# Linear attention and a squared-ReLU MLP on one core: padded v tails, paired tail divisions, fewer last stores, a second matmul by halves, a new order

## Chip, cores and metric

The kernel runs on one core of one Trainium2 chip. The metric is the device time of one execution in microseconds (us). The engines are TensorE (PE, with its weight loads shown as PEld), VectorE (DVE), ScalarE (ACT), GpSimd (POOL) and SyncE (SP). SP, ACT and POOL also issue DMAs.

## What is computed

```python
def _attn_ref(q, k, v):                  # 8 batches, 8 heads, 576 positions, 64 columns
    theta = np.pi / 2.0 * np.arange(S) / S
    cos_w, sin_w = np.cos(theta), np.sin(theta)
    phi = lambda x: concat([max(x, 0) * cos_w, max(x, 0) * sin_w], axis=-1)
    q_p, k_p = phi(q), phi(k)
    kv = np.einsum('bhsf,bhsd->bhfd', k_p, v)
    z = np.sum(k_p, axis=2)
    num = np.einsum('bhsf,bhfd->bhsd', q_p, kv)
    den = np.einsum('bhsf,bhf->bhs', q_p, z)[..., None] + 1e-06
    return num / den

def _moe_ref(x, w_in, w_out):            # 4608 tokens, 512 -> 2048 -> 512
    r = np.maximum(x @ w_in, 0.0)
    return (r * r) @ w_out
```

The attention's result, with the heads side by side, is the input x of the MLP. Inputs and output are float32; the matmuls run on bfloat16.

## The kernel before

**Tiling.** The 576 positions of a batch are 512 main ones (four tiles of 128, j = 0 to 3) and a tail of 64. The main positions of a batch go through the MLP as two token blocks of 256. The eight tails, 512 tokens, are gathered and go through the MLP as a ninth batch, number 8 in the names. In a tail tile heads 0 to 3 lie in partitions 0 to 63 and heads 4 to 7 in partitions 64 to 127.

**Stages of a batch.** Loads of q, k and v (`ldq`, `ldk`, `ldv`, and `ldqt`, `ldkt` for tails); features (`cos`, `sin`, with `.t` for the tail) into `fe` and `fet`; v cast to bfloat16 beside a column of ones (`vs`, into `vext` and, for the tail, `vextt`), so that one matmul gives kv and z; the sums (`kv`, into `kz` in PSUM, then copied to `kvz`); the transposed features of q (`qTd` by a DMA transpose, or `qT` and `qTc` by PE and a copy for batches 0 and 1) into `qpT` and `qpTt`; the numerators (`num`) and the division (`div`: add epsilon, reciprocal, multiply) into `xp` and `xpt`; and the transpose of x (`xTd` or `xT`, `xTc`) into `xT` and, for the tails, `xTt`.

**The MLP.** The first matmul is `H` (plain: batches 0 and 1 and half of batch 2) or `G` (a seven-product scheme after Strassen and Winograd, with sums `xs` of x blocks and `w1s` of weights). Its results are clipped (`...r`) and squared (`...q`) into `gT`. The second matmul is `Y0` (plain, batch 0) or `Yb` (seven products `P1` to `P7`, sums `S1` to `S4`, copies `seed`, `u2`, `s5`, results `c11` to `c22`, stores `st`).

**The order.** All of this is recorded first as named operations with the buffers that they use. Then the table `ORDER` (lines 23 to 116) is walked: it says in which order they are written out, and a star puts an operation on ACT instead of DVE. Each engine, and each DMA queue, runs its own instructions in that order. Buffers come from small pools (`pool(...)`): an operation that needs a new buffer is held until the last user of the old one is done. A pool of one, such as `pool("qpTt", 1, 1024)`, `pool("fet", 1, 2048)` and `pool("xpt", 1, 512)`, ties one batch to the one before it. SP's queue carries nearly all loads from batch 3 on, all DMA transposes and the stores; half of the very last stores are on ACT's.

**Lines that the change touches.** `mm_kv` (the tail is a matmul of 64 rows for each head: `fet[b][p0:p1, ...]` by `vxt[p0:p1, ...]`), `mm_num` (the tail's result fills 64 partitions for each half of the heads, in one PSUM bank), `div`, `spread_v` (v's casts), `x_dma`, `plan_q`, `plan_first2` (`Y0`: sixteen contraction blocks, each with four token tiles of 128), `store` and `plan_pair` with `apart=True` (the last `Y8`: 16 stores of 64 KB, in groups of two token tiles, two halves of heads, two column halves and two row blocks). All matmuls go through the helper `mm`, so they all carry its line, L459, and are told apart by their tiles.

Of the kernel before, what the change touches and what calls it, by code (L numbers as in the profile page):

```python
# [23 lines left out]
qT0.2 xT0.k2 xT0.k3 xTc0.k3* H0.0.00.0 xTc0.k2* qT0.3 qTc0.3* qTc0.2 num0.2 H0.0.00.1 H0.0.00.2  # L24
div0.2 H0.1.00.0 H0.1.00.1 H0.1.00.2 num0.3 div0.3 xT0.2 H0.0.00r* H0.3.00.0 H0.2.00.0 xT0.3
xTc0.3 xTc0.2* H0.0.01.0 H0.0.01r* H0.3.10.0 H0.3.10r H0.2.10.0 f0.t1* H0.0.10.0 H0.0.10r*
ldv2.0 H0.2.01.0 H0.2.01r* f0.t0 qT0.4 H0.2.00r* H0.1.00r H0.1.10.0 H0.1.10r* H0.1.10q H0.1.01.0
H0.0.11.0 H0.1.11.0 H0.1.01r* H0.1.00q qTc0.4* num0.4 H0.2.10r* H0.0.11r H0.3.00r* H0.2.11.0
H0.3.00q* H0.2.11r H0.3.01.0 H0.3.11.0 H0.3.01r* H0.1.11r H0.1.01q* Y0.0 sin1.t* div0.4 xT0.4
Y0.1 Y0.2 Y0.3 cos1.t* xTc0.4 H0.3.11r* qT1.4 qTc1.4* cos1.0 sin1.0* sin1.2 cos1.2* H0.3.10q  # L30
Y0.4 Y0.5 Y0.6 cos1.1 vs1.1* sin1.1 qT1.0 qTc1.0* cos1.3 Y0.7 vs1.0 sin1.3 qT1.3 qTc1.3* vs1.2
kv1 qT1.1 qTc1.1* qT1.2 H0.1.11q Y0.8 ldv2.2 w1s1 H0.3.11q* ldk2 ldq2 w1s2 ldkt2.0 ldkt2.1 kvz1
num1.1 ldkt3.0 div1.1 w2t1 qTc1.2* ldqt3.1 Y0.9 Y0.10 ldqt2.0 xT1.1 num1.2 Y0.11 div1.2 ldqt2.1
H0.3.01q* Y0.12 xTc1.1* w2t2 num1.0 div1.0 xT1.2 xTc1.2* vs2.2* ldkt3.1 Y0.13 Y0.14 num1.3
div1.3 vs2.0* xT1.0 xTc1.0* ldv3.2 Y0.15 H1.3.00.0 Y0.c11 Y0.c10* H1.3.00r* Y0.c00* ldv2.1
# [6 lines left out]
H1.2.11r* H1.3.11q Y1.S1 H1.3.01.0 Y1.P1 H1.3.01r* H1.3.01q* num2.0 div2.0 xTd2.0 Y1.S2 Y1.seed
Y1.P2 Y1.c11* num1.4 div1.4 Y0.st1 cos3.0 Y1.P6 sin3.1 Y1.S3 cos3.1* qTd2.2 sin3.0* qTd3.0
sin3.3 cos3.3* cos3.2* sin3.2 qTd3.1 vs3.1* Y1.P5 Y1.s5 xs2.1 Y1.S4 H2.1.10.0 H2.1.10r* sin3.t
ldk4 ldv4.0 ldkt4.0 H2.0.00.0 H2.0.01.0 H2.0.00r* H2.0.01r* xs2.2 G2.2.P1 H2.1.00.0 H2.1.00r*
H2.1.00q* cos3.t H2.0.11.0 ldq4 w1s4 Y1.u2* H2.0.11r xs2.4 kv3 G2.2.seed kvz3* vs4.2* ldv5.2
ldqt4.1 H2.1.11.0 xs2.3 w2t4 G2.2.P2 G2.2.c11r* num3.0 div3.0 H2.1.01.0 H2.1.01r* H2.1.01q
H2.1.11r* H2.1.11q* H2.0.10.0 H2.0.10r* ldkt4.1 num3.1 xT1.4 Y1.P7 H2.1.10q* div3.1 w1s3 xTd3.0
num3.2 div3.2 Y1.P3 vs4.0* G2.2.P5 G2.2.s5* num3.3 ldqt4.0 Y1.c22 Y1.c12 xTc1.4 G2.2.P6 G2.2.u2*
div3.3 G2.3.P1 G2.2.P3 G2.2.c12r G2.3.seed ldv4.1 G2.2.P7 sin4.0* num2.4 G2.3.P6 G2.3.u2* sin4.3  # L50
G2.3.P2 G2.3.c11r* G2.3.P5 G2.3.s5* xTd3.1 Y1.P4 qTd3.2 cos4.0 cos4.1 sin4.1 qTd4.0 G2.3.P7
G2.3.c11q G2.3.P3 Y1.st0 sin4.2* cos4.3* cos4.2* Y2.P1 G2.2.c22r G2.2.P4 cos4.t* G2.3.c22r
G2.3.P4 div2.4 Y1.c21* vs4.1 G2.3.c21r* qTd4.1 G3.0.P1 sin4.t kv4 G3.0.seed G2.2.c21r* kvz4*
ldv5.0 xs3.1 xs3.2 Y2.seed G3.0.P5 G2.3.c12r G2.3.c12q G3.0.P2 G3.0.c11r* xs3.4 ldq5 G2.3.c21q
G3.0.P6 G3.0.u2 xs3.3 G3.1.P1 G3.1.seed num4.0 div4.0 ldqt5.0 Y2.P2 G2.3.c22q* Y2.S1 G3.0.P7
G3.0.s5* G3.0.c22r G3.1.P2 G3.1.c11r* G3.1.P6 G3.0.P3 ldk5 Y2.S2 G3.1.u2* num4.2 div4.2 G3.0.P4
G3.1.P7 G3.1.P5 G3.0.c21r* Y2.S3 G3.0.c12r xTd2.2 G3.2.P1 Y2.P6 ldkt5.0 G3.1.c11q* num4.1
Y2.c11* div4.1 Y2.S4 ldkt5.1 Y2.P5 Y1.st1 vs5.0* G3.1.s5* G3.1.P3 G3.1.c12r num4.3 G3.1.c22r
ldqt7.0 div4.3 xTd4.0 Y2.u2* G3.2.P5 G3.2.s5* Y2.P7 G3.2.seed ldv5.1 G3.1.P4 Y2.s5* cos5.0*
G3.2.P6 sin5.3* G3.2.P2 G3.2.c11r* sin5.1 G3.1.c21r num3.4 G3.3.P1 cos5.1 cos5.2 Y2.P3 G3.3.seed  # L60
G3.3.P2 G3.3.P6 G3.2.u2* ldqt5.1 sin5.2 G3.2.P7 cos5.3 G3.1.c21q* Y2.c12 G3.3.u2* G3.3.c11r*
xTd4.1 G3.3.P5 Y2.c22 Y2.P4 G3.1.c22q* G3.3.s5* G3.1.c12q* sin5.0 qTd4.2 G3.2.c22r G3.2.P4
div3.4 G3.3.c11q qTd5.1 qTd5.0 vs5.1 ldv6.0 G3.3.P7 G3.3.c22r G3.2.P3 G3.2.c12r G3.3.P3
G3.3.c12r Y2.c21* G3.2.c21r* G4.0.P1 G4.0.seed G3.3.P4 Y3.P1 xs4.1 xs4.2 G4.0.P6 xs4.4
G3.3.c21r* G3.3.c21q* cos5.t* sin5.t G4.0.u2* G4.0.P5 G4.0.s5* vs5.2 G4.1.P1 xs4.3 G4.1.seed
G3.3.c12q G3.3.c22q kv5 Y3.S1 kvz5* ldkt7.1 G4.0.P3 G4.0.c12r G4.0.P2 G4.0.c11r* ldq6 num5.0
div5.0 G4.1.P6 G4.1.u2* G4.0.P7 G4.0.c22r G4.1.P5 Y3.seed G4.1.P7 vs6.0* Y3.S2 Y2.st1 G4.1.P2
num5.2 ldqt6.0 div5.2 ldk6 Y3.P2 G4.1.s5* G4.1.c22r ldkt6.1 G4.1.P3 num5.3 div5.3 Y3.c11* Y3.P6
G4.1.c11r* Y3.u2* cos6.2* G4.2.P1 G4.1.c11q* Y3.S4 G4.0.P4 G4.0.c21r Y3.P5 Y2.st0 ldkt6.0 Y3.S3
num5.1 div5.1 ldv6.1 G4.1.P4 G4.1.c21r* Y3.s5* G4.1.c12r G4.2.P5 xTd3.2 Y3.P7 G4.2.seed G4.2.s5  # L70
cos6.1* num4.4 G4.2.P3 xTd5.1 G4.1.c21q* G4.3.P1 G4.2.P2 G4.2.c11r* G4.2.P6 G4.1.c22q Y3.c22
Y3.P4 div4.4 G4.2.u2* G4.2.P7 G4.3.seed G4.3.P6 ldqt6.1 sin6.1 Y3.c21* G4.3.u2* cos6.0 sin6.2*
G4.1.c12q ldv6.2 G4.3.P5 sin6.3 qTd5.2 G4.3.P2 sin6.0 G4.3.P7 ldqt7.1 Y3.P3 cos6.3 vs6.2 G4.3.s5
xTd5.0 qTd6.0 G4.3.c11r* sin6.t G4.3.P3 vs6.1* cos6.t* qTd6.1 G4.2.c22r G4.2.P4 G4.3.c11q*
G4.3.c22r G4.2.c12r Y3.c12 G4.3.P4 G5.0.P1 G4.2.c21r* G5.0.seed kv6 xs5.1 Y3.st0 G4.3.c21r
G4.3.c21q* G5.0.P5 xs5.2 G5.0.P6 ldv7.0 G5.0.P2 kvz6* G5.0.s5* G4.3.c22q G5.0.c11r* G4.3.c12r
Y4.P1 Y4.seed num6.0 G5.0.u2 Y3.st1 G5.1.P1 G5.0.P3 Y4.P2 G4.3.c12q Y4.S1 Y4.S2 div6.0 G5.1.seed
G5.1.P2 G5.1.c11r* xTd4.2 vs7.0* G5.1.P6 G5.1.u2* xs5.3 num6.1 G5.0.P7 Y4.P6 Y4.S4 G5.1.c11q*
G5.1.P7 div6.1 Y4.S3 num6.2 xs5.4 ldk7 div6.2 ldq7 Y4.c11* G5.1.P5 G5.1.s5* Y4.u2* Y4.P5 Y4.s5*
# [203 lines left out]
def kernel(  # L283
# [812 lines left out]
    def plan_pair(b, apart=False):  # L1096
# [117 lines left out]
        for t in range(2):  # L1214
            plan_store(b, key, ys[1], 1, [e22], t, 1)
# [312 lines left out]
```

## Time and profile before

| | |
|---|---|
| median of 3 runs | 275.24 us (274.66 to 276.22) |
| the profiled execution | 275.57 us |
| its span, first to last instruction | 273.0 us |
| granted TensorE clock | 0.998 |
| PE busy | 265.0 us, 97% |
| DVE busy | 227.2 us, 83% |
| ACT busy | 186.9 us, 68% |
| last dense matmul starts in the group at | 267.16 us |
| DMA moved | 53.00 MB, mean 194 GB/s |

All times below count from the start of the span. PE's matmuls overlap in the pipeline: what a group costs is read from its start to the start of the next. "Idle before" stands in brackets with the instruction that ended it. A group's name is its output tile, an arrow, and its inputs: `kz<-vextt,fet` is the tail part of kv, `num<-kvz,qpTt` a tail numerator.

### The profile page before, as it was taken

The page shows a single profiled execution, that of the slowest core. Times are in us where ns is not written, and L with a number is a line of the kernel's source. Part 1 is how long each engine was busy: PE and PEld are TensorE (multiplying, and loading weights), DVE is VectorE, ACT ScalarE, POOL GpSimd, SP SyncE. Part 2 cuts the span into 40 slices and gives each one's busy share as a digit, 9 for nine tenths or more (in the row PEclk, how much of TensorE's full clock was granted, in tenths as well). Part 3 has the DMA queues.
Part 4 walks back from the last instruction along what each step waited for, and adds up shares of the span by engine and source line. Part 5 has one row for each costly group of instructions (what it writes and reads, how often), then busy time and mean ns, then how long its engine had stood idle before and what let it go on. Part 6 is the DMA issues. An engine that isn't in the chain of part 4 may idle for free.

```text
span 273.0 us, 6796 instructions
## 1 busy us (share of the span) xinstructions
PE 265.0 (97%) x2788; PEld 225.0 (82%) x2792; DVE 227.2 (83%) x412; ACT 186.9 (68%) x287; POOL 29.1 (11%) x47
## 2 busy tenths in 40 slices
PE   8999999999999989999999999999999999999992
PEld 3578756798899878989888998889988888888882
DVE  2773598897999989999999998998979979788931
ACT  5673888788699878699668866997249355747510
POOL 8934437100000000000000000000000000000000
PEclk9999999999999999999999999999999999999999
DMA  7999999999999999999993999573150010100125
GB/s 223 311 206 271 317 284 319 297 248 346 197 274 326 184 254 262 345 227 259 366 204 88 271 323 246 145 208 46 41 192 4 10 77 3 79 0 2 74 70 166
DMA packets 79198, 53.00 MB, mean 194 GB/s; under 512 B 52256, under 2 KB 74784, under 8 KB 79168
## 3 DMA queue, kind: packets, MB, share of 16 engines
q1 hardware_dynamic: 71488, 38.28, 55.3%
q0 software_dynamic: 7040, 13.76, 19.0%
q10 hardware_dynamic: 640, 0.52, 0.7%
q8 instruction: 22, 0.36, 0.6%
q14 instruction: 8, 0.07, 0.1%
HBM read 36.70 MB, written 9.44 MB: 169 GB/s over the span
## 4 chain that ended last, share of the span: by engine, by line
PE 91%; ACT 2%; DMA 2%; POOL 2%; issue 1%; DVE 0%; POOLq 0%; ACTq 0%
PE ya L459 19%; PE yb L459 15%; PE hps L459 13%; PE hb L459 12%; PE hc L459 8%; PE ha L459 8%; PE yh L459 5%; PE num L459 4%; PE kz L459 3%; DMA v<-in_v_dram 2%; PE yc L459 1%; PE tq L609 1%; ACT fe L446 1%; PE tx L614 1%; PE wm L459 1%
## 5 line engine op out<-in xcount | busy, mean ns | idle before, releaser
L459 PEld LDWEIGHTS <-w1sb 128*128 128x128 bf16 x736 | 70.6, 98 | 8.7 <-DMA w1sb<-in_moe_w_in_dram 0.2
L459 PEld LDWEIGHTS <-gs 128*128 128x128 bf16 x512 | 49.7, 98 | 5.7
L459 PEld LDWEIGHTS <-gT 128*128 128x128 bf16 x448 | 43.3, 98 | 10.3 <-issue 0.5
L440 ACT ACTIVATE gT<-gT 128x1024 bf16<-128x1024 bf16 x39 | 41.1, 1058 | 3.0 <-DVE gT L453 2.7
L459 PE MATMUL hps<-xT,w1sb 128*128 128x256 bf16 x320 | 37.6, 273 | 0.0
L459 PEld LDWEIGHTS <-w1s 128*128 128x128 bf16 x312 | 29.7, 98 | 4.2 <-issue 0.6
L448 DVE TENSOR_SCALAR fe<-kq,cols 128x1024 bf16<-128x1024 f32 (+1 forms) x43 | 28.8, 712 | 4.1 <-DMA kq<-in_k_dram 4.1
L459 PE MATMUL ya<-w2sb,gT 128*128 128x256 bf16 x256 | 30.7, 273 | 0.4 <-ACT yb L430 0.4
L459 PE MATMUL hb<-xs,w1sb 128*128 128x256 bf16 x208 | 30.1, 272 | 0.0
L446 ACT ACTIVATE fe<-kq,cols 128x1024 bf16<-128x1024 f32 (+1 forms) x29 | 28.7, 1032 | 2.0 <-DMA kq<-in_k_dram 2.0
L459 PE MATMUL ha<-xT,w1sb 128*128 128x256 bf16 x176 | 25.8, 273 | 0.0
L442 DVE TENSOR_TENSOR gT<-gT 128x1024 bf16<-128x1024 bf16 x33 | 22.1, 686 | 2.8 <-ACT gT L434 2.6
L591 DVE TENSOR_TENSOR xp<-num,den 128x512 bf16<-128x512 f32 (+1 forms) x33 | 22.2, 675 | 1.1
L453 DVE CUSTOM_DVE_ANT_0 gT<-hb,s 128x512 bf16<-128x512 f32 x26 | 17.6, 687 | 5.3 <-PE hb L459 5.0
L434 ACT ACTIVATE gT<-hps 128x512 bf16<-128x512 f32 x30 | 17.0, 597 | 6.7 <-PE hps L459 6.6
L434 ACT ACTIVATE gT<-ha 128x512 bf16<-128x512 f32 x23 | 13.8, 601 | 9.9 <-PE ha L459 9.9
L456 DVE TENSOR_TENSOR gs<-gT 128x2048 bf16<-128x2048 bf16 x16 | 19.5, 1220 | 0.7 <-ACT gT L440 0.2
L453 DVE CUSTOM_DVE_ANT_0 gT<-hc,u 128x512 bf16<-128x512 f32 x26 | 17.5, 684 | 1.1 <-PE hc L459 0.7
L430 ACT COPY hb<-ha 128x512 f32<-128x512 f32 x26 | 15.2, 584 | 2.8 <-PE ha L459 2.6
L459 PE MATMUL hc<-xs,w1s 128*128 128x256 bf16 x104 | 15.6, 273 | 0.7 <-ACT gT L434 0.7
L459 PE MATMUL hb<-xs,w1s 128*128 128x256 bf16 x104 | 15.4, 273 | 0.0
L459 PE MATMUL yb<-w2t,gs 128*128 128x256 bf16 x128 | 15.3, 273 | 0.0
(112 smaller groups left out, 410.1 us busy)
## 6 DMA issues: line engine op xcount, KB each, us to landing
out_dram<-y SPq DMA_DIRECT2D x16, 512.0 KB, 3.8
vs<-in_v_dram SPq DMA_DIRECT2D x10, 512.0 KB, 5.5
kq<-in_q_dram SPq DMA_DIRECT2D x5, 1024.0 KB, 7.6
kq<-in_k_dram SPq DMA_DIRECT2D x5, 1024.0 KB, 7.4
w1sb<-in_moe_w_in_dram POOLq DMA_DIRECT2D x4, 512.0 KB, 11.1
w2sb<-in_moe_w_out_dram POOLq DMA_DIRECT2D x4, 512.0 KB, 10.7
kq<-in_q_dram POOLq DMA_DIRECT2D x2, 1024.0 KB, 11.9
kq<-in_k_dram POOLq DMA_DIRECT2D x2, 1024.0 KB, 9.7
```

The lines of the kernel that those rows point to most:

```text
L430: (nc.scalar.copy if e == "ACT" else nc.vector.tensor_copy)(out=out, in_=in_)
L434: nc.scalar.activation(out=out, in_=in_, func=ACTF.Relu)
L440: nc.scalar.activation(out=out, in_=in_, func=ACTF.Square)
L442: nc.vector.tensor_tensor(out=out, in0=in_, in1=in_, op=ALU.mult)
L446: nc.scalar.activation(out=out, in_=in_, func=ACTF.Relu, scale=col)
L448: nc.vector.tensor_scalar(out=out, in0=in_, scalar1=0.0, scalar2=col, op0=ALU.max, op1=ALU.mult)
L453: nc.vector._custom_dve(dve_ops.TENSOR_ADD_SAT, out=out, in0=in0, in1=in1, s0=BIG, s1=0.0)
L456: nc.vector.tensor_tensor(out=out, in0=in0, in1=in1, op=op)
L459: nc.tensor.matmul(out=out, lhsT=lhsT, rhs=rhs, start=start, stop=stop, skip_group_check=True)
L591: nc.vector.tensor_tensor(out=x, in0=n4[:, :, :, 0:D].rearrange("p b (k l) d -> p b k l d", l=2), in1=r.rearrange("p b (k l) -> p b k l", l=2)
L609: nc.tensor.transpose(t[:, h, :], src, ident[:, :])
L614: nc.tensor.transpose(t[:, kb, :], src, ident[:, :])
```

## The change

The v tail, `vextt`, becomes two copies of full height: copy g holds the values of its half of the heads in its 64 partitions, and zeros elsewhere. The tail part of kv is then a matmul over all 128 partitions, in which the zeros cancel the other half. The tail numerators of an even batch wait for those of the odd batch after it: both fill one pair of PSUM banks and one division handles them; one transpose moves both. For this, `qpTt` has two buffers, `kvz` three and `xpt` twice the size. `Y0` is planned as two halves of two token tiles each, `Y0.a` and `Y0.b`, which the table interleaves. The last `Y8` stores two token tiles at once except for the last block, so there are ten stores instead of sixteen, and its product `P4` is no longer split. The sum `w1s3`, which overwrites part of w1, waits for fewer plain products, and `w2t3` for the last readers of the upper half of w2 in both halves of `Y0`. The table `ORDER` is a new one throughout.

```diff
-    pool("qpTt", 1, 1024)
+    pool("qpTt", 2, 1024)
-    pool("xpt", 1, 512)
+    pool("xpt", 1, 1024)
-    pool("kvz", 2, 1088)
+    pool("kvz", 3, 1088)
...
-    vxt = sb.tile([P, HH, E1 + 7], BF16, name="vextt", tag="vxt", bufs=1)
+    vxt = sb.tile([P, 2, HH, E1 + 7], BF16, name="vextt", tag="vxt", bufs=1)
+    sides = [slice(g * TAIL, (g + 1) * TAIL) for g in range(2)]
-    nc.vector.memset(vxt[:, :, D:E1], 1.0)
+    nc.vector.memset(vxt, 0.0)
+    for g in range(2):
+        nc.vector.memset(vxt[sides[g], g, :, D:E1], 1.0)
...
+    def spread_tail(e, src):
+        for g in range(2):
+            copy(e, vxt[sides[g], g, :, 0:D], src[sides[g]])
...
-                        p0, p1 = half * TAIL, (half + 1) * TAIL
-                        lhsT, rhs = fet[b][p0:p1, 0, hh, :], vxt[p0:p1, hh, 0:E1]
+                        lhsT, rhs = fet[b][:, 0, hh, :], vxt[:, half, hh, 0:E1]
...
     def mm_num(num, b, j):
+        if j == J:
+            for i in range(2):
+                mm_num_tail(num[i], b - 1 + i)
+            return
...
+    def mm_num_tail(num, b):
+        for hh in range(HH):
+            for half in range(2):
+                e0, h, s_ = hh * E1, half * HH + hh, sides[half]
+                o, lhsT = num[s_, e0 : e0 + E1], qpTt[b][:, hh, s_]
                 mm(o, lhsT, kvz[b][:, h * E1 : (h + 1) * E1], True)
...
-                ds.append(num_div(b, j, [kc, qt], [qb]))
+                if j == J:
+                    tails[b] = [kc, qt]
+                    if not b % 2:
+                        return
+                    held = [qb, qpTt[b - 1], kvz[b - 1]]
+                    ds.append(num_div(b, j, tails[b] + tails[b - 1], held))
+                else:
+                    ds.append(num_div(b, j, [kc, qt], [qb]))
...
+        read = []
         for i in range(2):
+            ys = [buf("x", [P, DM], F32, "yh", "full") for _ in range(2)]
+            last = None
+            for hb in range(HB):
+                def emit(e, hb=hb, i=i, ys=ys):
+                    for t in range(2):
+                        g = gT[0, i, hb // HB2][:, hb % HB2, t, :]
+                        mm(ys[t][:, :], g, w2sb[:, hb, :], hb == 0, hb == HB - 1)
...
-        for t in range(2):
-            plan_store(b, key, ys[1], 1, [e22], t, 1)
-        for t in range(2):
-            plan_store(b, key, ys[0], 0, [e12], t, 1)
+        plan_store(b, key, ys[1], 1, [e22], None, 1)
+        plan_store(b, key, ys[0], 0, [e12], None, 1)
+        p4 = prod(4, Bb, block(1, 1), lambda: w2t[4], False, [e22, w[4]], [run])
+        e21 = ev("c21", flex(2), lambda e: copy(e, left(1), bank(run)), [p4], [run, ys[1]])
+        plan_store(b, key, ys[1], 1, [e21], None, 0)
         for t in range(2):
-            for m, i, lhs, rhs, acc, o in (
-                (4, 1, block(1, 1), lambda: w2t[4], [run], Bb),
-                (2, 0, block(0, 1), lambda: w2_block(1, 0), accs[t : t + 1], A),
-            ):
+            lhs = block(0, 1)
+            p = prod(2, A, lhs, lambda: w2_block(1, 0), False, seeds, accs[t : t + 1], t, t + 1)
...
+            plan_store(b, key, ys[0], 0, [e], t, 0)
...
-                w2_in + [made[a] for a in after] + ([plain] if n == 3 else []),
+                w2_in + [made[a] for a in after] + (plain if n == 3 else []),
...
-                            plains += plan_plain1(b, s_, tok, half)
+                            them = plan_plain1(b, s_, tok, half)
+                            plains += them if half else []
```

Two places of the new table that the prediction speaks of (batch 3's transposed q tails, and the end; the old table has `qTd3.2` between `xTd3.1` and `sin4.t`):

```
... kvz3* H2.1.00q num3.0 H2.1.11r* G2.2.P2 div3.0 qTd3.2 H2.1.01.0 ... xTd3.0 G2.3.P1 ... xTd3.1 G2.2.P3 ...
... Y8.st011 Y8.st001 Y7.P4 Y8.c22 Y8.st101 Y8.P4 Y7.c21 Y8.st111 Y7.st1 Y8.P20
Y8.c21 Y8.P21 Y8.c110* Y8.st100 Y8.st110 Y8.st0000 Y8.st0010 Y8.c111 Y8.st0100 Y8.st0110
```

More of the change, by code (lines that the diff above doesn't have):

```diff
@@ L42 @@
[L42 to L47, printed above, removed]
@@ L1366, in begin @@
                 values(0)
-                copy("DVE", vxt[:, :, 0:D], vt0[:, :, :])
+                spread_tail("DVE", vt0)
         warm(2, "x0")
```

295 lines of the change are left out of this document (143 added, 152 removed).

## The prediction

> **What bounds the kernel now.** I read the page first (parts 1 and 2), then TensorE (PE) in order of time, the waits, and the windows where PE is not full.
>
> ```profile
> PE 265.0 (97%) x2788; PEld 225.0 (82%) x2792; DVE 227.2 (83%) x412; ACT 186.9 (68%) x287; POOL 29.1 (11%) x47
> ...
> PE   8999999999999989999999999999999999999992
> ```
>
> PE is busy in every slice but the first and the last. Between its first dense matmul (16.5 us) and the last one (268.2) only PE's own instructions and rare gaps count. So three things can shorten the run: fewer PE slots, a gap removed, a shorter end. The gaps are seen in the windows (columns: stretch, length, then busy us and instructions of PE, PEld, DVE, ACT, POOL, clock, DMA share, GB/s).
>
> ```profile
> 90.00:100.00 10.00, 10.00 (x120) 8.87 (x118) 8.55 (x18) 7.69 (x11) 0.00 (x0) 1.00 1.09 177
> 100.00:110.00 10.00, 9.30 (x112) 8.19 (x109) 9.54 (x19) 8.98 (x17) 0.00 (x0) 1.00 1.08 285
> 110.00:120.00 10.00, 10.00 (x110) 8.82 (x108) 9.76 (x18) 7.74 (x13) 0.00 (x0) 1.00 1.24 293
> ```
>
> VectorE (DVE) is almost as full as PE there: 9.5 to 9.8 of 10. The timeline of PE gives the price of a slot (start, duration, instruction; durations overlap, so cost is read from start to start).
>
> ```profile
> 60.64 1.13 PE L459 MATMUL kz<-vext,fe 128*128 128x65 bf16 x32
> 61.70 0.29 PE L459 MATMUL kz<-vextt,fet 64*128 64x65 bf16 x8
> 61.93 1.05 PE L459 MATMUL hps<-xT,w1sb 128*128 128x256 bf16 x8
> 62.81 0.41 PE L459 MATMUL num<-kvz,qpT 128*128 128x65 bf16 x8
> 63.05 1.91 PE L459 MATMUL hps<-xT,w1sb 128*128 128x256 bf16 x16
> ...
> 91.56 0.60 PE L459 MATMUL hb<-xs,w1sb 128*128 128x256 bf16 x4
> 92.09 0.32 PE L459 MATMUL num<-kvz,qpTt 128*64 128x65 bf16 x8
> 92.34 0.61 PE L459 MATMUL hb<-xs,w1s 128*128 128x256 bf16 x4
> ```
>
> A full 65-column matmul costs 0.24/8 = 0.030 us (62.81 to 63.05), a 256-column one 1.75/16 = 0.109.
>
> **The change, part by part.** (1) *Padded v tails.* kv now takes 61.93 - 60.64 = 1.29 us. Its 32 full matmuls should take 32 x 0.030 = 0.96, but the half-height ones start after 1.06: 0.10 goes at the switch. The eight half-height ones and the way back take 0.23. Padded to full height it is 40 x 0.030 = 1.20, so 0.09 less for each of batches 1 to 7: **-0.63**. Bounds: nothing, if the switch belongs to the first 32; and -0.91, if a full one costs 0.029 when forty follow each other (1.16). The trace's half-height forms lie at the row itself, so I take -0.63.
>
> The Trainium skill, "TensorEngine Tiling (Array Packing)", Theoretical Speedup, speaks against this part: contractions of 64 rows run as two tiles side by side, up to twice as fast, which padding gives up. Its Key Properties add that changing the tiling mode drains the engine. The trace has both (0.10 at the switch, 0.23 for the eight) and the drain outweighs the packing at eight matmuls. By the first rule alone eight padded ones would cost 0.12 more a batch, and the sum would be 1.47 us higher.
>
> (2) *Tail numerators and divisions of two batches.* A tail group now starts 0.09 late (91.56 + 0.44 = 92.00, starts 92.09), takes 0.25, and delays what follows by 0.01: 0.35, eight times, 2.80. Sixteen at once: 0.09 + 16 x 0.030 + 0.02 = 0.59, four times, 2.36: **-0.44** (bounds -0.2 to -0.7, since the cost of a switch is read to 0.05 at each of eight places). DVE: 8 x (0.154 + 0.178 + 0.424) = 6.0 becomes 4 x (0.163 + 0.203 + 0.691) = 4.2, the longer durations being those of the main divisions. v's tail copy becomes two of half the partitions and the same length: +0.29 in three batches on DVE, and on ACT +0.40 in four, covered by ACT's 32% idle time. DVE gains about 1 us in all, off the path. The transposed tails of x go out as three double transfers for six; batch 8's products, which read them from 229.6 on, are the first to need them, so this is hidden. Transposes on PE are as many as before.
>
> (3) *A second buffer for the transposed q tails.* This removes the one long gap:
>
> ```profile
> 96.29 1.22 SPq L627 DMA_TRANSPOSE qpTt<-fet  x1
> ...
> 99.72 0.72 ACT L446 ACTIVATE fet<-kqt,cols 128x512 bf16<-128x512 f32 x1 [2.01 <-issue]
> ...
> 101.46 0.60 PE L459 MATMUL hc<-xs,w1s 128*128 128x256 bf16 x4 [0.67 <-ACT gT L434]
> ```
>
> The features of batch 4's tail (99.72, ACT, idle 2.0 before them) overwrite what batch 3's transfer of 96.29 reads, and it lands about 3.3 us after issue (the median of this kind). That transfer could not stand earlier, because the only buffer was held until batch 2's tail numerators at 92.09. Behind the waiting ACT instruction stand a copy and the activation for which PE waits until 101.46; PE should have gone on at 100.50 + 0.23 = 100.73, and the kv tail itself came 0.10 late. **-0.83** (bounds 0, if the new order puts another wait there, to -0.9). In the new table this transfer stands right after batch 3's first numerators, ahead of both transfers of x, so ACT finds the buffer free. Even batches still wait for the previous pair's numerators, but those lie some 10 us ahead of the features that need the buffer.
>
> (4) *Fewer last stores.* The last copy is done at 268.65, but:
>
> ```profile
> 268.23 0.42 DVE y L430
> ```
>
> ```profile
> 269.81 0.47 SPq L1047 DMA_DIRECT2D out_dram<-y  x1
> ```
>
> ```profile
> 270.00 0.47 ACTq L1047 DMA_DIRECT2D out_dram<-y  x1
> ```
>
> (chain of waits; DMA issues of SP; of ACT). Both queues have 8 stores of 64 KB; the order of instructions shows that each must wait until an earlier DMA of its semaphore, eight DMAs back, has landed (median 2.8 us), and a wait of SP ends at 269.8. With 5 and 5 stores, those earlier ones were issued before 264 and the wait goes. What is then late next is the queue itself: on ACT the copy of the first half ends at about 267.75, and three issues of 0.69 (median there) put the last one at 269.1, against 270.00. **-0.9** (bounds 0, if landing and not issue holds the end, to -1.2, when issues cost 0.5). Landing, 3.0 us to 273.0, stays.
>
> (5) *Batch 0's second matmul by halves.* The same 64 matmuls, and PE is gapless from 21.74 to 50: **0**. Cover: the fifth of the sixteen contraction blocks needs the second quarter of w2, issued at 25.75 and landed 10.3 later (36.05 or, from the issue's end, 36.8). PE reached it at 36.59; now batch 0's tail work (0.45) is gone from ahead of it, so it comes at 36.15: cost 0 to +0.45.
>
> (6) *Startup.* DVE's second v tail copy adds 0.40 at 11.53, so the second half of v ends at 13.07 instead of 12.67 and the second kv group starts at 13.10 instead of 12.89. It takes 20 x 0.030 = 0.60 instead of 0.83 and ends when it did: **0** (bounds 0 to +0.25). The longer memset (+0.25, by the zeros memset, 0.27) hides in ACT's idle 1.64 us before 4.72.
>
> (7) *The new table.* Other gaps of PE (0.2 at 21.5, 0.5 at 70.0, 0.15 at 19 and at 107) sum to 1.0. The one at 70 remains: the seed copy still lies between the first and second product of batch 1, with one numerator group as cover. For the rest I take as much as before, **0**; bounds -0.5 to +4 (below).
>
> Sum: -0.63 - 0.44 - 0.83 - 0.9 = **-2.8**. The profiled execution took 275.57 (span 273.0, 2.57 around it), 0.33 above the median, so it would go to 272.8 with a span of 270.2, and the median from 275.24 to **272.5**.
>
> **Rivals.** *A. The order gives it back (within 0.5%).* Parts 1, 2 and 4 hold (-2.0), but the new order has 1.8 us more of small waits, as many as the old one has in all: 275.0. For it: the old order, written out just as long, shows 1.8 us of gaps in the trace. Against: nearly half of those have one cause, which goes.
>
> *B. Slower: DVE sets the pace between 92 and 160 us.* There it is 9.5 to 9.8 of 10 busy, and counting the new table with these durations it gets as much DVE work from batch 4's kv to batch 5's (18 us for PE's 18). Wherever a square, a division or an add stands one place too early, its DVE successor is late and PE waits for the PSUM bank, as in the window 100 to 110 (0.8 us). Five of the seven windows with such a gap: -2.0 + 5 x 0.83 = +2.1: 277.4. It decides from 2.0 + 1.4 = 3.4 us of gaps on. Against: all windows but one have PE at 10.00 with the same load.
>
> *C. More.* Full-height kv at 1.16, issues at 0.5, gaps down by 0.5: -0.91 - 0.6 - 0.9 - 1.2 - 0.5 = -4.1: 271.1.
>
> *D. Packing mattered.* If the half-height ones now run in pairs, eight cost four slots, 0.12; padded they cost eight, 0.24; with no switch saved, part 1 is 7 x 0.12 = +0.84 instead of -0.63 and the time 274.0. Only the row 61.70 (0.23 with the way back) speaks on it, and against it. This is the case of the Trainium skill's speedup rule named above.
>
> That the change doesn't do what it says: the last two stores could still wait for their semaphores; then -0.9 goes and the time is 273.4.
>
> **How the numbers follow.** Forecast 0.50 (own range 271.6 to 273.8), C 0.11, D 0.03, A 0.17, B 0.19. A measurement of this kernel tells about 0.5% (1.4 us) from no change: the three runs before span 1.56. Faster (below 273.9): 0.50 + 0.11 = 0.61. Same: 0.03 + 0.17 = 0.20. Slower (above 276.6): 0.19. The range leaves out B's upper part and C's lower one: 271.0 to 276.6.
>
> **What would show it.** kv groups of 40 equal matmuls in 1.20 us; four tail groups of 16 in 0.5; no 2 us of idle ACT before the tail features; the last stores issued within 0.6 us of the last copy; PE at 10.00 in the windows of 90 to 160. Wrong would be: PE waits for DVE or ACT over 2.5 us in sum, a wait for w2 near 36, or stores that still end near 270.

## The result, and the profile after

The changed kernel takes 273.13 us (median of 6 runs, 272.79 to 274.37). The kernel before, measured beside it, takes 275.48 (6 runs, 274.66 to 276.22). The ratio is 0.9924, 95% interval 0.9897 to 0.9951: 0.8% faster. By the medians that is 2.35 us, by the ratio 2.1, where 2.8 had been forecast; the time, 273.13, lies 0.6 above the forecast 272.5.

The profiled execution of the changed kernel took 273.90, 0.77 more than its median, with a span of 271.8. The page, parts 1 and 2:

```profile
PE 263.3 (97%) x2787; PEld 224.4 (83%) x2792; DVE 226.7 (83%) x403; ACT 187.6 (69%) x292; POOL 28.9 (11%) x47
...
PE   8799999999999999999999999999999999999994
```

PE is busy for 1.7 us less and is as full as before. PE in order of time (start, duration, instruction, as in the prediction) shows the two steps that shorten its work: kv, and a pair of tail numerators.

```profile
60.87 1.13 PE L461 MATMUL kz<-vext,fe 128*128 128x65 bf16 x32
61.84 0.40 PE L461 MATMUL kz<-vextt,fet 128*128 128x65 bf16 x8
62.08 1.04 PE L461 MATMUL hps<-xT,w1sb 128*128 128x256 bf16 x8
...
98.12 0.60 PE L461 MATMUL hb<-xs,w1sb 128*128 128x256 bf16 x4
98.65 0.45 PE L461 MATMUL num<-kvz,qpTt 128*64 128x65 bf16 x16
99.03 1.92 PE L461 MATMUL yb<-w2t,gT 128*128 128x256 bf16 x16
```

kv takes 62.08 - 60.87 = 1.21 (1.29 before); the tail's matmuls start 0.97 after the first instead of 1.06, so the pause at the change of height is gone. Sixteen tail numerators take 99.03 - 98.65 = 0.38, with 0.09 before and 0.01 after them 0.48.

The gap at 100 us is gone. Windows (columns as in the prediction):

```profile
90.00:100.00 10.00, 10.00 (x117) 8.73 (x115) 9.67 (x19) 9.59 (x15) 0.00 (x0) 1.00 1.16 280
100.00:110.00 10.00, 10.00 (x105) 9.00 (x104) 8.89 (x16) 7.45 (x14) 0.00 (x0) 1.00 1.07 265
```

PE is busy for ten us of ten in both, where before the second had 9.30. But there is a new gap at 80 us. PE, ACT and SP's queue in order of time:

```profile
74.20 0.45 PE L461 MATMUL num<-kvz,qpTt 128*64 128x65 bf16 x16
...
78.08 3.06 PE L461 MATMUL hps<-xT,w1sb 128*128 128x256 bf16 x24
81.98 1.91 PE L461 MATMUL hps<-xT,w1sb 128*128 128x256 bf16 x16 [0.83 <-ACT gT L436]
```

```profile
80.72 0.72 ACT L448 ACTIVATE fet<-kqt,cols 128x512 bf16<-128x512 f32 x1 [2.17 <-DMA qpTt<-fet]
81.35 0.58 ACT L436 ACTIVATE gT<-hps 128x512 bf16<-128x512 f32 x1
```

```profile
70.89 3.51 SPq L649 DMA_TRANSPOSE xT<-xp  x1
74.51 0.52 SPq L512 DMA_DIRECT2D vs<-in_v_dram  x1
75.13 2.24 SPq L649 DMA_TRANSPOSE xT<-xp  x1
77.46 1.22 SPq L640 DMA_TRANSPOSE qpTt<-fet  x1
```

It is the gap of 100 us over again, one batch earlier: batch 3's tail features (80.72) overwrite what the transfer of batch 2's transposed q tails (77.46) reads. That transfer could not go out earlier for two reasons: its buffer was held by batch 0's tail until the first pair of numerators (74.20 to 74.58), and then it stood in SP's queue behind two transfers of x and a load, until 77.46. The square for which PE waits at 81.98 stands behind those features on ACT. From kv of batch 2 to kv of batch 3, start to start, the kernel takes 23.29 us; a run below (a_best) shows 22.02 for the same work without the wait, so the gap costs 1.27 in this execution.

The end, SP's and ACT's queues and the last copy:

```profile
267.10 1.97 SPq L1069 DMA_DIRECT2D out_dram<-y  x3
267.25 0.37 ACT L432 COPY y<-ya 128x256 f32<-128x256 f32 x1 [9.02 <-PE ya L461]
267.32 1.99 ACTq L1069 DMA_DIRECT2D out_dram<-y  x3
268.13 0.42 DVE L432 COPY y<-ya 128x256 f32<-128x256 f32 x1 [1.06 <-PE ya L461]
```

The last copy is done at 268.55, and the issue of the last store ends at 269.31. From the end of that copy to the end of the span it is 3.25, where it was 4.35.

Where the profiled 273.0 - 271.8 = 1.2 of span went (from PE's starts):

| stretch | before | after | difference |
|---|---|---|---|
| span's start to kv of batch 1 (the old one has 0.35 of tail numerators in it) | 40.94 | 41.25 | +0.31 |
| kv of batch 1 to the end of PE's last matmul | 227.26 | 226.84 | -0.42 |
| from there to the end of the span | 4.80 | 3.71 | -1.09 |
| around the span | 2.57 | 2.10 | -0.47 |

In the second row seven kv give -0.56, the tail numerators (7 x 0.35 became 4 x 0.48) -0.53, the gap at 100 us about -1.0, and the new one at 80 us +1.27: -0.8, where the row shows -0.4. The run a_unpad below shows where the other 0.4 went.

### The profile page after: what moved, and what is told of

It reads as the page before. It is cut to its first block, busy times and chain, and to the rows that moved or that the text cites. A ratio compares the mean times of both kernels' runs of the same rounds, so it can differ in the third digit from the quotient of the medians.

```text
span 271.8 us, 6753 instructions
## 1 busy us (share of the span) xinstructions
PE 263.3 (97%) x2787; PEld 224.4 (83%) x2792; DVE 226.7 (83%) x403; ACT 187.6 (69%) x292; POOL 28.9 (11%) x47
## 4 chain that ended last, share of the span: by engine, by line
PE 84%; DMA 6%; DVE 4%; POOL 3%; issue 1%; ACT 0%; SPq 0%; POOLq 0%; ACTq 0%
PE ya L461 17%; PE yb L461 14%; PE hb L461 13%; PE hps L461 10%; PE hc L461 8%; PE ha L461 8%; PE yh L461 5%; DMA w1sb<-in_moe_w_in_dram 5%; PE kz L461 3%; PE num L461 3%; PE yc L461 1%; DVE gs L458 1%; DMA qpTt<-fet 1%; PE tq L622 1%; DVE fe L450 1%
## 5 line engine op out<-in xcount | busy, mean ns | idle before, releaser
L442 ACT ACTIVATE gT<-gT 128x1024 bf16<-128x1024 bf16 x38 | 39.6, 1060 | 4.0 <-DVE gT L455 2.0
L450 DVE TENSOR_SCALAR fe<-kq,cols 128x1024 bf16<-128x1024 f32 (+1 forms) x44 | 30.1, 722 | 5.2 <-DMA kq<-in_k_dram 3.5
L448 ACT ACTIVATE fe<-kq,cols 128x1024 bf16<-128x1024 f32 (+1 forms) x28 | 27.6, 1027 | 2.9 <-DMA kq<-in_k_dram 1.6
L461 PE MATMUL ha<-xT,w1sb 128*128 128x256 bf16 x176 | 26.4, 273 | 0.0
L444 DVE TENSOR_TENSOR gT<-gT 128x1024 bf16<-128x1024 bf16 x34 | 23.0, 687 | 1.6 <-ACT gT L436 1.3
L436 ACT ACTIVATE gT<-hps 128x512 bf16<-128x512 f32 x27 | 15.6, 595 | 6.4 <-PE hps L461 6.4
L436 ACT ACTIVATE gT<-hb 128x512 bf16<-128x512 f32 x20 | 11.9, 601 | 6.7 <-PE hb L461 6.6
```

Of the source, the lines that this page charges most:

```text
L436: nc.scalar.activation(out=out, in_=in_, func=ACTF.Relu)
L442: nc.scalar.activation(out=out, in_=in_, func=ACTF.Square)
L444: nc.vector.tensor_tensor(out=out, in0=in_, in1=in_, op=ALU.mult)
L448: nc.scalar.activation(out=out, in_=in_, func=ACTF.Relu, scale=col)
L450: nc.vector.tensor_scalar(out=out, in0=in_, scalar1=0.0, scalar2=col, op0=ALU.max, op1=ALU.mult)
L461: nc.tensor.matmul(out=out, lhsT=lhsT, rhs=rhs, start=start, stop=stop, skip_group_check=True)
```

## The experiments

Each kernel was timed beside the kernel before on the same chip, in three groups, each on another chip: a_unpad, a_stores16, a_apart and a_q2early (before: 275.58, 29 runs); a_best, a_whole, b_q3early and b_parts (275.89, 32 runs); a_whole2, b_pad, b_padmm and b_stores10 (275.37, 35 runs). So the ratio to before is what compares across groups; a ratio of 0.001 is 0.28 us. The changed kernel itself was timed only once, with an interval of 0.9897 to 0.9951: where the interval of an "a_" kernel overlaps it, the times alone do not show a difference. "a_" starts from the changed kernel, "b_" from the one before.

**a_unpad: v's tail back in one copy.**

```diff
-        for g in range(2):
-            copy(e, vxt[sides[g], g, :, 0:D], src[sides[g]])
+        copy(e, vxt[:, :, 0:D], src[:, :, :])
...
-                        lhsT, rhs = fet[b][:, 0, hh, :], vxt[:, half, hh, 0:E1]
+                        s_ = sides[half]
+                        lhsT, rhs = fet[b][s_, 0, hh, :], vxt[s_, hh, 0:E1]
```

> The changed kernel with the v tail back in one copy and the tail part of kv back to half-height matmuls; all else as changed, the same order. My theory: the padding saves what the change of tile height costs, so the kv group of batches 1 to 7 goes from 1.21 us back to 1.29 and the time rises by 7 x 0.08 = 0.56 us, to about 273.7 against 273.13. Rival (packing): two half-height matmuls side by side are worth 0.12 us a batch, so the kernel gets up to 0.84 us faster. A third: the second copy of v's tail on DVE and its longer clearing cost up to 0.5 us at the start (the first dense matmul at 17.64 us before the change, 18.14 after), and come back here: the time then stays within 0.1 us of the changed kernel's and the first dense matmul is at 17.6 again.

Measured: 274.01 us (12 runs, 273.14 to 274.88), ratio 0.9937 (0.9913 to 0.9962), 0.0013 above the changed kernel. Its PE in order of time:

```profile
61.58 1.13 PE L459 MATMUL kz<-vext,fe 128*128 128x65 bf16 x32
62.64 0.30 PE L459 MATMUL kz<-vextt,fet 64*128 64x65 bf16 x8
62.87 1.05 PE L459 MATMUL hps<-xT,w1sb 128*128 128x256 bf16 x8
```

kv is back at 1.29, and the half-height matmuls start 1.06 after the first. The difference in time (0.36 by the ratios, 0.9 by the medians) is in line with 7 x 0.08 = 0.56, but the intervals overlap. A gain of 0.84 from leaving the padding out, which packing would have given, is not there. Nor does the start show the third idea: the twelve dense matmuls that start at 18.14 in the changed kernel start at 17.88 here, and at 17.78 to 17.82 in three other kernels with padding.

The profile also shows that padding loses most of its gain again. From kv of batch 3 to the start of PE's last group the changed kernel takes 182.02 (84.16 to 266.18) and a_unpad 182.10; five kv of 0.08 less would make 0.40. PE loses 0.37 at two places that a_unpad lacks. The first, ACT and PE in the changed kernel:

```profile
86.94 0.82 ACT L432 CAST vextt<-vst 64x256 bf16<-64x256 f32 x2
87.78 0.60 ACT L436 ACTIVATE gT<-ha 128x512 bf16<-128x512 f32 x1
```

```profile
87.79 0.60 PE L461 MATMUL hb<-xs,w1s 128*128 128x256 bf16 x4
88.42 0.38 PE L627 MATMUL tx<-ident,xpt 128*128 128x128 bf16 x4
```

and in a_unpad:

```profile
86.67 0.40 ACT L430 CAST vextt<-vst 128x256 bf16<-128x256 f32 x1
86.97 0.60 ACT L434 ACTIVATE gT<-ha 128x512 bf16<-128x512 f32 x1
```

```profile
87.53 0.60 PE L459 MATMUL hb<-xs,w1s 128*128 128x256 bf16 x4
87.97 0.39 PE L625 MATMUL tx<-ident,xpt 128*128 128x128 bf16 x4
```

Two copies of v's tail take 0.82 on ACT, one takes 0.40. The activation behind them, which empties the PSUM tile `ha`, ends at 88.38, and PE's next group starts 0.04 later, 0.63 after the one before it, where four such matmuls cost 0.44. In a_unpad the activation ends at 87.57 and PE goes on without a pause. At 137.63 the same happens again (0.18), behind the two copies of 136.15. The other kernels with padding in the new order take the same 182.0 for this stretch (a_apart, which has 0.67 more for another reason, aside). So the new order pays for the second copy too.

**a_stores16: the paired last stores cut in two again**, with everything else as changed.

```diff
+        if c is not None and t is None:
+            for u in range(2):
+                plan_store(b, key, y, i, after, u, c)
+            return
```

> The changed kernel with each of its six last stores of two token tiles (128 KB) split in two of 64 KB: 16 last stores as before the change, in the new order. My theory: with 16 the last ones stand behind the landing of DMAs eight places back, and behind each other's issue; the last one is issued 1.2 to 1.4 us after the last copy instead of 0.2, and the time rises by 1.0 to 1.2 us, to about 274.2. Rival: landing, not issue, holds the end (3.1 us from the last issue to the end in both profiles): then the last issue is later but the end moves by less than 0.4 us.

Measured: 274.34 us (12 runs, 272.69 to 276.04), ratio 0.9946 (0.9917 to 0.9975). The end of its profile, with a span of 273.9:

```profile
268.63 2.40 SPq L1069 DMA_DIRECT2D out_dram<-y  x4
...
268.85 2.50 ACTq L1069 DMA_DIRECT2D out_dram<-y  x4
269.66 0.42 DVE L432 COPY y<-ya 128x256 f32<-128x256 f32 x1 [1.06 <-PE ya L461]
```

Each queue has four stores instead of three behind the last products, and ends 0.4 to 0.5 later against the copy; from the copy's end (270.08) to the span's end it is 3.82, against 3.25. (The span of 273.9 holds a larger gap at 80 us as well: 24.94 from kv of batch 2 to kv of batch 3.) So the number of stores is worth 0.57 of the 1.10 that the end gained, by one profile against one. That is half of what was expected. In the times the difference is 0.6 by the ratios and 1.2 by the medians, and the intervals overlap.

**a_apart: the two batches' tail numerators apart**, with one MLP product between them.

```diff
-... Y1.P2 div2.0 ldv3.1 Y1.P6 ... num1.4 ...
+... Y1.P2 div2.0 ldv3.1 num1.4a Y1.P6 ... num1.4 ...
```

The other three pairs are cut in the same way.

> The changed kernel with each group of sixteen tail numerators cut in two groups of eight, with one full-height product of the MLP between them. Division and transposes stay paired. My theory: what the pairing saves on PE is one change of tile width and back, read from start to start as 0.09 + 0.25 + 0.01 = 0.35 us for eight and 0.09 + 0.38 + 0.01 = 0.48 for sixteen, so each pair costs 0.22 us more: the time rises by 4 x 0.22 = 0.9 us, to about 274.0. The prediction as written (only 0.11 a pair): 0.44 us, to 273.6. Rival: the pairing is worth its DVE time alone, and the time does not move.

Measured: 274.85 us (12 runs, 274.05 to 276.6), ratio 0.9964 (0.9938 to 0.999), 0.0040 above the changed kernel. PE in order of time:

```profile
74.68 0.32 PE L461 MATMUL num<-kvz,qpTt 128*64 128x65 bf16 x8 [0.74 <-DVE xp L603]
...
99.39 0.32 PE L461 MATMUL num<-kvz,qpTt 128*64 128x65 bf16 x8
99.64 0.61 PE L461 MATMUL hb<-xs,w1sb 128*128 128x256 bf16 x4
100.18 0.32 PE L461 MATMUL num<-kvz,qpTt 128*64 128x65 bf16 x8
100.44 1.81 PE L461 MATMUL yb<-w2t,gT 128*128 128x256 bf16 x15
```

Each eight take 0.25 (99.39 to 99.64) again, with the 0.10 around them 0.35: two of them 0.70, against 0.48 for sixteen together. So a pair is worth 0.22, four pairs 0.88. From kv of batch 3 to the start of PE's last group, where the other three pairs lie, the kernel takes 182.69 instead of 182.02: 0.67, three times 0.22. In the stretch of the first pair, my place for the first half made a wait of 0.74, but ACT's wait for the transfer is gone there, and the stretch is 23.05 instead of 23.29. So the rows bear out the price, against the 0.44 of the prediction; the time fits it less surely, since the intervals overlap.

**a_q2early: batch 2's tail transfer moved up** from behind `cos3.0` to right behind `kv2`, with a third buffer for it. (v's tail copies get shorter rows, `E1 + 1` for `E1 + 7`, to make room.)

```diff
-    pool("qpTt", 2, 1024)
+    pool("qpTt", 3, 1024)
...
-... w2t4 kv2 ldv3.2 ... Y1.P5 cos3.0* qTd2.2 sin3.0 ...
+... w2t4 kv2 qTd2.2 ldv3.2 ... Y1.P5 cos3.0* sin3.0 ...
```

> The changed kernel with a third buffer for the transposed q tails (and 6 unused columns of each v tail head left out, to make room), and batch 2's transfer into it put right behind batch 2's kv in the order, some 16 us earlier. My theory: the tail features of batch 3 on ACT wait 2.17 us for that transfer's landing at 80.6, the activation behind them releases a PSUM bank late, and PE stands still for about 1.3 us in sum between 79.8 and 82.0; with the transfer early, that wait and the PE gaps go and the time falls by 1.0 to 1.3 us, to about 272.0. Rival: ACT and DVE are the bound there (DVE 9.5 of 10), so PE waits for the next square instead and the time falls by less than 0.4 us.

Measured: 272.75 us (6 runs, 271.94 to 274.15), ratio 0.988 (0.9838 to 0.9922). SP's queue, and PE:

```profile
61.50 1.23 SPq L640 DMA_TRANSPOSE qpTt<-fet  x1
```

```profile
80.54 2.78 PE L461 MATMUL hps<-xT,w1sb 128*128 128x256 bf16 x24 [0.21 <-DMA xT<-xp]
```

The transfer now goes at 61.50 instead of 77.46, ACT no longer waits for it, and kv of batch 2 to kv of batch 3 takes 22.39 instead of 23.29: 0.9 won in the profile. In the times it is 0.4 by the medians and 1.2 by the ratios, whose intervals overlap. What is left is a wait for the transfer of x.

**a_best: in addition two loads and a cast of v moved** behind batch 2's transfers of x (`ldv4.2` behind `xTd2.1`, `ldv3.1` behind `xTd2.0`, `vs3.1` behind `div1.4`).

> The kernel with batch 2's tail transfer moved up (the q2early run), and in addition two loads and a cast of v near 70 to 80 us moved behind batch 2's transfers of x in SP's queue. Theory: what is left of the gap at 80 us (0.2 to 0.3 on PE, ended by the landing of x's transfer) is late because the transfers stand behind loads in SP's queue; 0.2 to 0.4 less than the q2early run, a median near 272.4 and a span near 270.9. Rival: the transfer's landing is set by the traffic and not by its place in the queue; then the wait on the landing stays and the time is that of the q2early run, 272.75, within 0.2.

Measured: 272.92 us (9 runs, 272.24 to 274.97), ratio 0.9918 (0.9885 to 0.9951); the profiled execution took 272.86, with the shortest span of all profiled ones, 270.7. Its windows:

```profile
70.00:80.00 10.00, 9.64 (x106) 8.41 (x106) 9.83 (x16) 7.02 (x10) 0.00 (x0) 1.00 1.11 270
80.00:90.00 10.00, 9.97 (x135) 8.97 (x133) 9.39 (x20) 7.40 (x13) 0.00 (x0) 1.00 1.04 298
```

The changed kernel has 9.63 and 9.02 there. The wait is gone and the stretch is down to 22.02. In the times nothing more than in a_q2early shows, and the ratio is that of the changed kernel (0.9918 and 0.9924). The intervals of all three overlap, so no version here is shown to beat it, though both profiles lack its gap.

**a_whole: batch 0's second matmul whole again**, each block at the later of its halves' two places.

```diff
-... Y0.b8 Y0.b9 qTc1.2* num1.1 Y0.b10 div1.1 ldqt2.1 Y0.a8 H0.3.01q* Y0.a9 ...
+... qTc1.2* num1.1 div1.1 ldqt2.1 Y0.8 H0.3.01q* Y0.9 ...
```

> The changed kernel with batch 0's second matmul whole again: every contraction block at the later of the places that its two halves have in the new order. Theory (term 5: the halves are worth nothing): the same time within 0.3, 273.1, and PE without gaps from 23 to 52 us. Rival: the halves let PE take up the second matmul while the other half's squares or w2's second quarter are still under way; then a wait of 0.5 or more shows before 52 us and the time is 273.6 or more.

Measured: 276.8 us (12 runs, 275.93 to 278.05), ratio 1.0034 (1.0009 to 1.0058): 0.011 above the changed kernel, 3 us, and slower than before. PE:

```profile
44.10 0.42 PE L459 MATMUL num<-kvz,qpT 128*128 128x65 bf16 x8 [0.70 <-ACT qpT L430]
...
48.80 0.42 PE L459 MATMUL num<-kvz,qpT 128*128 128x65 bf16 x8 [1.22 <-DVE xp L602]
```

Where the changed kernel has half blocks (three matmuls ahead of the first numerators), nothing covers the copy of transposed q and, later, the division: 1.92 us of waits. That is most of the 2.6 by which PE's last group starts later in the profile; the rest is in no single place (0.35 in the same stretch, 0.4 in the stretch to kv of batch 3).

**a_whole2: the same, with each block where the order has reached half of its pair.**

```diff
+... Y0.8 qTc1.2* num1.1 div1.1 ldqt2.1 Y0.9 H0.3.01q* ...
```

> The changed kernel with batch 0's second matmul whole, each block where the new order has reached half of its two halves (between the first and the second of the pair), so that PE has about the same work ahead of every numerator. Theory, formed on the first run with whole blocks: that run lost 1.9 us because its blocks came too late to cover the copies of transposed q and a division, not because they were whole; placed so, the waits of 0.70 and 1.22 between 44 and 49 us shrink below 0.5 in sum and the time is that of the changed kernel within 0.5 (273.4). Rival: a block of 0.87 is too coarse, and only halves let 0.43 to 0.87 of work stand in each of these places; over 0.7 of waits remains there.

Measured: 274.59 us (12 runs, 273.43 to 275.76), ratio 0.9967 (0.9947 to 0.9986). In the profile the stretch from kv of batch 1 to kv of batch 2 takes 19.62 (41.44 to 61.06), as in the changed kernel (41.25 to 60.87), and no wait is left in it. So in the first run the places had cost the 1.92, not the size of the blocks. But the expected time, that of the changed kernel within 0.5, did not come: the times put this kernel 0.0043 above the changed one, 1.2 us (the intervals barely overlap), and the profiled execution, the fastest of the twelve, does not show where. What the halves are worth beyond their places stays open.

**b_q3early: the old kernel with a second buffer, and batch 3's tail transfer moved up** to right behind `kv3`.

```diff
-    pool("qpTt", 1, 1024)
+    pool("qpTt", 2, 1024)
...
-... kv3 G2.2.seed ... xTd3.1 Y1.P4 qTd3.2 cos4.0 ...
+... kv3 qTd3.2 G2.2.seed ... xTd3.1 Y1.P4 cos4.0 ...
```

> The old kernel with its old order, given only the second buffer for the transposed q tails, and batch 3's tail transfer moved up to right behind batch 3's kv. Theory (term 3 of the prediction): the 2.0 us in which ACT stood idle before batch 4's tail features go, and the gap of PE near 100 us with them: -0.83 in the profile, a median near 274.7. Rival 1, the one that the changed kernel showed with another pair of batches: another wait for the same transfer takes the gap's place, less than 0.3 is won. Rival 2: what the changed kernel spends less outside its span (0.33) comes with the smaller queue waits and would show here too.

Measured: 274.79 us (12 runs, 274.11 to 275.67), ratio 0.9972 (0.9948 to 0.9996), that is -0.77 (-1.4 to -0.1). Windows:

```profile
90.00:100.00 10.00, 10.00 (x110) 8.82 (x108) 9.46 (x21) 8.97 (x13) 0.00 (x0) 1.00 1.22 206
100.00:110.00 10.00, 10.00 (x132) 9.02 (x129) 9.83 (x18) 8.40 (x15) 0.00 (x0) 1.00 1.07 303
```

kv of batch 4 to kv of batch 5 takes 28.39 instead of 29.41; from kv of batch 1 on every other stretch, from kv to kv and to PE's end, is the same to 0.01. The theory holds, and nothing takes the gap's place here. The size is less sure than the 1.02 suggests, for the gap differs from profile to profile: with the old buffer and the old place of the transfer, the stretch takes 29.67 in b_stores10 and 28.82 in b_pad, and in b_padmm 28.30, without any gap. The times, -0.77, are the better measure. The second rival holds in part: outside the span this kernel spends 2.31 (median), where before spends 2.56 in the same group. But b_parts, with the same buffer and the same place, spends 2.56.

**b_pad: the old kernel with the padded tails alone**, and **b_padmm: full-height matmuls over the one old copy.** In b_padmm there are no zeros, so each head's tail sum also takes in the other half's rows; only the tail matmuls of kv (56 in batches 1 to 7, eight in batch 0) differ from before.

```diff
-                        p0, p1 = half * TAIL, (half + 1) * TAIL
-                        lhsT, rhs = fet[b][p0:p1, 0, hh, :], vxt[p0:p1, hh, 0:E1]
+                        lhsT, rhs = fet[b][:, 0, hh, :], vxt[:, half, hh, 0:E1]    # b_pad
+                        lhsT, rhs = fet[b][:, 0, hh, :], vxt[:, hh, 0:E1]          # b_padmm
```

> The old kernel in its old order with the padded v tails alone: two copies of v's tail for one, 40 full-height matmuls a batch. Theory, formed on the run of the three parts together (which lost what the parts should have won): in the old order the second copy of the tail, 0.3 on DVE or 0.4 on ACT a batch, comes out of engines that PE waits for; kv is 0.08 shorter in seven batches, but 1 to 2 us of small waits of PE come in between 18 and 90 us and the time is that of before or up to 1.2 more. Rival: padding is worth its -0.56 here too and the loss of the three parts came from the stores' new end; then about 0.5 less than before.

> The old kernel with full-height tail matmuls of kv over the one old copy of v's tail: no zeros and no second copy, so that each head's tail sum also takes in the rows of the other half of the heads. Only the 56 matmuls differ. Theory: the matmuls alone are worth -0.56 (7 x 0.08), because nothing is added on DVE or ACT; the difference to the run with both copies is the price of the second copy in the old order, 0.6 to 1.8. Rival: a PE that is faster by 0.08 a batch meets DVE and ACT too early and waits; then the time is that of before within 0.2.

Measured: b_pad 275.74 us (12 runs, 275.1 to 277.27), ratio 1.0014 (0.9995 to 1.0033), +0.4; b_padmm 274.87 us (12 runs, 273.8 to 276.15), ratio 0.9984 (0.9963 to 1.0004), -0.4. Neither is shown to differ from before: the interval of b_padmm holds the theory's -0.56 and the rival's 0. But the two were timed side by side, and b_pad takes 0.8 more by the ratios (the means are 275.85 and 274.98, and the difference is well beyond their scatter). That is the price of the second copy in the old order. The profiles show it between kv and kv, start to start (kv of batch 4 to that of batch 5 holds the gap at 100 us and is left out):

| batches | 1 to 2 | 2 to 3 | 3 to 4 | 5 to 6 | 6 to 7 |
|---|---|---|---|---|---|
| before | 19.70 | 20.24 | 18.46 | 24.05 | 29.18 |
| b_padmm | 19.92 | 20.14 | 18.40 | 23.95 | 29.09 |
| b_pad | 19.85 | 20.51 | 18.61 | 24.30 | 29.37 |

In four of the five stretches the full-height matmuls alone win 0.06 to 0.10, about the 0.08 of their rows; with the second copy the same stretches lose 0.15 to 0.27.

**b_stores10: the old kernel with ten last stores and P4 whole.**

```diff
-Y8.st1001 Y8.P40 Y8.c210 Y8.P20 Y8.P41 Y8.st1101 Y7.c21* Y7.st1 Y8.st1011 ...
+Y8.st101 Y8.P4 Y7.c21* Y8.st111 Y7.st1 Y8.P20 Y8.c21 Y8.P21 Y8.c110* Y8.st100 ...
```

> The old kernel in its old order with ten last stores and P4 whole, nothing else. Theory (term 4): the end of the span comes 0.6 to 1.1 earlier after the last matmul (4.8 before, 3.7 in the changed kernel), a median of 0.6 to 1.1 less than before, and the time outside the span stays at 2.5. Rival: the end is won by the new order's other changes, 0.3 or less here.

Measured: 275.03 us (12 runs, 274.27 to 276.58), ratio 0.9994 (0.9973 to 1.0014). From the last copy's end to the span's end: 3.76 here and 3.59 in b_parts (ten stores each), 4.35, 4.04, 3.73 and 4.15 in before, b_q3early, b_pad and b_padmm (sixteen). The means are 3.68 and 4.07: 0.4 in the old order, with a spread as large as that. The theory's 0.6 to 1.1 is not reached, neither at the end nor in the time.

**b_parts: the old order with padded tails, ten stores and the early transfer together.**

> The old order with three parts of the change and nothing else of it: padded v tails, ten last stores with P4 whole, and the second buffer with batch 3's tail transfer moved up. Batch 0's second matmul stays whole and the tail numerators unpaired. Theory: the parts are worth their own prices in any order, -0.56 (kv tails as measured) -0.83 (gap) -0.6 to -1.1 (end) = -2.0 to -2.5, a median near 273.3, level with the changed kernel, though it lacks 0.88 of paired numerators, because it also lacks the new gap of 1.3 at 80 us. Rival: the parts need the new order (the planner's new table places the transfers for them); then less than half shows, 274.5 or more.

Measured: 275.44 us (12 runs, 274.56 to 276.91), ratio 0.9993 (0.997 to 1.0016), -0.2. The rival holds: less than half shows. The single runs add up to it, +0.4 - 0.2 - 0.8 = -0.6, within the interval. From kv of batch 1 to kv of batch 4 it needs 59.32 where b_q3early needs 58.40. Two of the three stretches, 20.51 and 18.61, are those of b_pad: the second copy again.

## Why the prediction was right, point by point

The time lies within the forecast range, but in part by luck. Two terms came out worse than forecast, the second buffer by 1.1 us and the startup by 0.7 in the profile; the numerators and the time outside the span came out better by 0.4 and 0.5.

1. *Padded v tails, -0.63.* The row is right: 1.21 for 1.29, -0.56 in seven batches. What was wrong is the cover: "on ACT +0.40 in four, covered by ACT's 32% idle time". A share of the whole span hides what an engine has to do where PE waits for it: at 88 and 137 us the second copy delays ACT's next instructions, and PE loses 0.37 there. So the change keeps about 0.2 of the 0.56 in the profile, and its time against a_unpad's is not clear of noise. In the old order the second copy cost 0.8, more than the matmuls win. Rival D (packing) falls by the rows of kv and by a_unpad, which is not faster.

2. *Paired numerators, -0.44.* Mis-sized: -0.88 (0.70 to 0.48, four times), above the bound of 0.7. I priced the further eight at the full-height row, 0.030 each. Eight take 0.25 and sixteen 0.38, so each of them costs 0.13 / 8 = 0.016, half a full one, and some 0.12 of each group belongs to the switch. The Trainium skill, "TensorEngine Tiling (Array Packing)", Theoretical Speedup and When to Use Tiling, gives up to twice the speed where the free dimension of LHS, here the stationary side, is at most 64, as here (128 by 64, the halves alternating). The trace agrees for the matmuls inside a group (0.016 against 0.030); the prediction read that rule for the rows of kv only. Whether the eight half-height kv matmuls were fast in the same way, and lost it to the pauses around them, no run shows: none has more than eight of them in a row.

3. *The second buffer, -0.83.* The gap at 100 us went, as predicted: -1.02 in b_q3early's profile, -0.77 in its times. But the sentence "Even batches still wait for the previous pair's numerators, but those lie some 10 us ahead of the features that need the buffer" failed. For batch 2 they lie at 74.20, and ACT was ready for the features at 78.55, 4.35 us later. The transfer goes out at 77.46, behind two transfers of x, lands 3.15 later and keeps ACT idle for 2.17, where "no 2 us of idle ACT" had been forecast. That cost 1.27 in the profiled execution. The bound "0, if the new order puts another wait there" was the case, one batch earlier. The cause is shown by a_q2early and a_best: with the transfer moved up, ACT's wait is gone. What the gap costs in a usual execution is open, for the times do not show those two kernels faster.

4. *Fewer last stores, -0.9.* The end is 1.1 shorter in the profile. The number of stores is 0.4 to 0.6 of it (b_stores10, a_stores16), by single profiles. SP's wait for an earlier store, on which the term was built, is 0.8 to 0.9 in the four profiles with the old end and gone in the changed kernel. But it is gone in a_stores16 too, which has sixteen stores: what sixteen cost there is one more issue in each queue. That the wait is for the DMA eight places back, no run shows. The rest comes with the new order of the end; one difference to be seen is that the old order and b_stores10 have a copy of batch 7 on ACT ahead of ACT's stores, the new one has not. Nothing was run on that alone.

5. *Batch 0's second matmul by halves, 0.* No wait for w2 came near 36 us, and whole blocks in places halfway show no wait either between kv of batch 1 and kv of batch 2 (a_whole2). But the places carry weight: these blocks are what covers the copy and the division at 44 and 49 us, and later places cost 1.9 there (a_whole).

6. *Startup, 0.* kv of batch 1 starts 0.31 later though 0.35 of numerators is gone from ahead of it: +0.7, above the bound of 0.25. That is one execution against one. Over the profiles of old-order kernels with one copy of v's tail this start lies between 40.67 and 41.37, and the two with two copies have 41.76 and 41.93; in the new order it is 41.1 to 41.4 with padding and 41.3 without (a_unpad), but 42.65 in a_apart, which waited 1.54 for w1. The terms of the startup are smaller than what w1's landing does to it: in the profiles of the new order PE waits 0.24 to 1.54 us for w1, a_whole aside, which shows no such wait.

7. *The new table, 0.* The gap at 80 us belongs here too: with the 0.37 behind the second copies, the new order gives back 1.6 in the profile, which is nearly what rival A said (1.8). It did not end at rival A's time because the numerators, the end and the time around the span brought more than their terms. Apart from that the table's waits are as small as those of before, and the seed copy still costs PE 0.36 at 70.61. Rival B (DVE sets the pace) falls: the windows of 90 to 160 us have 10.00 but for one of 9.98.

Sum: -0.56 - 0.88 - 1.0 - 1.1 + 1.27 + 0.7 + 0.37 = -1.2 inside the span, which is what it shows; with -0.47 around it that is the profiled executions' difference of -1.67. The medians differ by 2.35, because the profiled execution of the changed kernel lies 0.77 above its median and that of before 0.1. So the term that failed is the third. What made up for it is the second, which was mis-sized by half, and time outside the span, which was no term at all: that was luck.

## What to carry to other kernels

Give a shared buffer's next user a place in the queue by asking when the last reader of the old contents runs, for every batch and not for one: adding a buffer while two batches are paired moved the same wait one batch earlier. Do not count an added copy as covered because its engine is idle for a third of the span: look at what stands behind the copy on that engine and whether PE waits for it. Here the second copy took back 0.37 of 0.56 in the new order, and more than was won in the old one. And do not add up the prices of parts without a run of them together: padding, early transfer and fewer stores together won 0.2 in the old order (interval -0.4 to 0.8), where 2.0 to 2.5 had been expected.

## What was not expected of the hardware

- Matmuls with 64 columns in the stationary tile, alternating between the two halves, cost 0.016 us each inside a group of sixteen, half of the 0.030 of full ones; entering and leaving such a group costs about 0.2 in all (0.12 inside, 0.10 around it).
- The same transposing DMAs take very different times. In kernels with the same order around 80 us, the issue of batch 2's second transfer of x took 1.24 to 2.32, and ACT then waited 1.02 to 2.43 for the transfer behind it; PE's loss there went from 0.1 (a_unpad) to 2.9 (a_stores16), measured against the 22.02 of a_best. At 100 us of the old order it went from 0 (b_padmm) to 1.3 (b_stores10). Each kernel was profiled in one execution, so the size of such a gap in one profile says little about its mean.
- The time around the span fell from 2.5 to 2.1 in all kernels with the new order (medians 2.13 to 2.16), with ten stores or sixteen; those with the old order have 2.31 to 2.56. It is a sixth of the gain, and nothing run here tells its cause.
